# A four-layer transformer step on one core: the linear layer's numerators as sixteen 32x32 tiles, two scratch sets for VectorE, and a newly planned order

## The chip, the cores and the metric

One core of a Trainium2 chip runs the whole program. The metric is the device time of one execution in microseconds; the kernel before takes 2145.01 us (median of 3 runs, 2144.82 to 2145.63).

## The reference, cut to what matters

Two kinds of layers alternate, A, B, A, B, on one sequence of 2048 rows of 1024 elements, in bf16. Each has 32 heads of 32 elements, its layer norm ahead and a residual sum behind it. A is linear attention: a softmax feature map of q and k, a 64x32 state per head, and a quotient. B is full softmax attention.

```python
def _A_ref(x, wqkv, w_phi, wo):
    q, k, v = ...                                        # (B, 32 heads, S, 32)
    pq, pk = einsum("bhsd,hdf->bhsf", q, w_phi), einsum("bhsd,hdf->bhsf", k, w_phi)
    phi_q = concatenate([softmax(pq), softmax(-pq)], axis=-1)      # phi_k alike
    kv = einsum("bhsf,bhsd->bhfd", phi_k, v)
    z  = einsum("bhsf->bhf", phi_k)
    num = einsum("bhqf,bhfd->bhqd", phi_q, kv)
    den = einsum("bhqf,bhf->bhq", phi_q, z)[..., None] + 1e-6
    return (num / den).transpose(...).reshape(B, S, D) @ wo
def _B_ref(x, wqkv, wo):
    p = softmax(einsum("bhqd,bhkd->bhqk", q, k) * Dh ** -0.5)
    return einsum("bhqk,bhkd->bhqd", p, v).transpose(...).reshape(B, S, D) @ wo
x = x + _A_ref(layernorm(x), ...)
x = x + _B_ref(layernorm(x), ...)
x = x + _A_ref(layernorm(x), ...)
x = x + _B_ref(layernorm(x), ...)
```

## The kernel before, in words

The program runs the pair A, B twice (`layer` 0 and 1). The 2048 rows are four chunks `c` of 512. Activations stand transposed (channels on the partitions, rows along the free dimension), so that most matrix products are 128x128 by 512. Four heads fill 128 partitions; such a group of four is `g` in B, and `a` within a half `hf` in A's queries.

Nothing is ordered by hand. Each piece of work is recorded with its engine, a cost in microseconds, its buffers, the pieces it depends on and a priority (`Sched.op`). `Sched.run` then plays a clock through the five engines: whenever an engine is free, it takes the ready piece of lowest priority number whose buffers can be had, under quotas for each kind of buffer (`QUOTA`). The order in which pieces are taken is the order in which instructions are written for each engine. Some rules look at the state of that clock, and some pieces (the score products of B) are created while it runs. A page of constants sets priorities, distances and limits.

**A's keys** (`a_keys`, `a_state`): projections of k and v, exponentials, and the state `kv` and `z`. The state is put into `kvm` as block-diagonal 128x128 matrices (L895 zeroes it on POOL, L899 copies the blocks on VectorE).

**A's queries** (`a_queries`, for each chunk and half, four groups `a` of four heads): the projection (L600), two exponentials each (L972), the sums of them (L983), a ratio of the two softmax denominators through logarithms (L989 to L995) that `split_hl` and `spread` (L935) spread over the partitions, four multiplications on VectorE (L1000), and then for each `a` the numerators: two 128x128 by 512 products with `kvm` (L1010), copied out of PSUM by ScalarE (L1014). The denominators (L1021) go the same way through `spread`, and four multiplications (L1032) give the rows that `a_out` projects with `wo`.

**B's attention** (`attention`): work goes by turns, one turn being a chunk of queries `qc` and a group `g`, 32 turns per layer. A turn has 64 units, a unit being the scores of one head's 128 keys with 512 queries (L1209, a 32-row tile of the array). Scores of two or three units lie side by side in PSUM, and ScalarE turns them into exponentials with one instruction of 1024 or 1536 columns (L1267). A further unit per group can be given to VectorE: L1354 converts it, and for each pair of converted units a chain of four instructions finishes the exponential (`exp_dve`: two masks L1171 into `work`, a product L1176 into `work`, a sum L1176 out of `work`). `work` is one scratch set, held from the first mask to the sum (the buffer `xx`, with one place). TensorE multiplies the results with v and with ones (L1397), VectorE copies the sums out (L1412, twice a turn), and DMAs and VectorE make the quotient. Under the attention lie the projections of B's keys, queries and values (L604), and under that of layer 0 also three chunks of A's keys for layer 1. When TensorE has nothing to do, the planner lets it multiply constants (L604 with `onesD`, L1649, L1654).

How many units VectorE gets is decided while the order is planned, by VectorE's load and by the constants `MOST`, `MIX`, `LOAD`, `THIRD_LOAD`, `BOTH_LOAD`.

## Time and profile before

| what | us |
|---|---|
| median of 3 runs (lowest, highest) | 2145.01 (2144.82, 2145.63) |
| the profiled execution, its own time | 2143.52 |
| its span in the profile | 2141.7 |
| TensorE busy in the span | 2097.4 |
| ScalarE busy | 1929.9 |
| VectorE busy | 1720.8 |
| first and last start of a B exponential (L1267) | 319.1 and 2129.3 |

"Busy" of TensorE counts a product until its modelled end, and products overlap, so 98% does not say that it is full; how closely products follow each other does. Stages by the trace: A's keys to about 155 us, A's queries and B's first projections to 319, attention of layer 0 to about 1171, the rest of layer 1's A to about 1372, attention of layer 1 to 2131, and the last rows. In the attention the copies L1412 mark the turns: copy 1 starts at 345.1 us, copy 32 at 747.2, copy 48 at 958.3, copy 63 at 1160.9, copy 65 (layer 1) at 1401.1, copy 96 at 1769.5 and copy 126 at 2121.3.

### The profile page before, as it was taken

How to read it: one execution, taken by the hardware profiler on the slowest of the kernel's cores; microseconds unless marked ns; L12 is line 12 of the kernel's file. 1: busy time of each engine (PE TensorE's matmuls, PEld its weight loads, DVE VectorE, ACT ScalarE, POOL GpSimd, SP SyncE). 2: the span in 40 equal slices, each digit the busy share in tenths (PEclk: the TensorE clock that was granted, in tenths of full speed). 3: DMA queues.
4: the chain of work that ended last, by engine and by line, in shares of the span. 5: the costliest groups of instructions: out<-in, count | busy, mean ns of one | idle time of the engine just before them, and what ended most of it. 6: DMA issues, size and time to landing. Idle time of an engine off the chain costs nothing.

```text
span 2141.7 us, 64212 instructions
## 1 busy us (share of the span) xinstructions
PE 2097.4 (98%) x27375; PEld 795.1 (37%) x27437; DVE 1720.8 (80%) x3151; ACT 1929.9 (90%) x2044; POOL 27.4 (1%) x78
## 2 busy tenths in 40 slices
PE   8999999999999999999999999999999999999999
PEld 5543443333333333333333434533333333333333
DVE  8876553665567899997887876599899999999998
ACT  7437668999999999999999576799999999999998
POOL 1000000000000000000000000000000000000000
PEclk9999999999999999999999999999999999999999
DMA  7820321112233431451456212211111122311111
GB/s 233 164 71 20 86 63 32 32 42 49 65 99 85 123 107 52 120 154 47 108 154 194 78 40 69 70 28 31 36 49 38 45 53 54 84 39 52 54 44 37
DMA packets 255271, 160.73 MB, mean 75 GB/s; under 512 B 147592, under 2 KB 229512, under 8 KB 254984
## 3 DMA queue, kind: packets, MB, share of 16 engines
q1 hardware_dynamic: 254984, 156.62, 27.3%
q8 instruction: 214, 3.51, 0.7%
q14 instruction: 73, 0.60, 0.1%
HBM read 89.72 MB, written 29.87 MB: 56 GB/s over the span
## 4 chain that ended last, share of the span: by engine, by line
PE 57%; ACT 26%; DVE 9%; issue 5%; DMA 2%; POOL 0%; SPq 0%; ACTq 0%; DVEq 0%; POOLq 0%
ACT arena L1267 26%; PE psum L600 19%; PE psum L604 13%; PE psum L1397 11%; PE psum L1209 10%; DVE arena L1354 3%; DVE work L1171 1%; PE psum L1010 1%; DVE work L1176 1%; DVE arena L1176 1%; DMA arena<-rd 1%; DMA arena<-arena 1%; PE psum L855 1%; ACT arena L820 1%; PE psum L935 1%
## 5 line engine op out<-in xcount | busy, mean ns | idle before, releaser
L1267 ACT ACTIVATE arena<-psum 128x1536 bf16<-128x1536 f32 (+1 forms) x1343 | 1580.5, 1478 | 4.7 <-PE psum L1209 2.9
L604 PE MATMUL psum<-arena 128*32 128x512 bf16 (+1 forms) x9536 | 633.1, 365 | 4.2 <-DVE arena L816 1.0
L1397 PE MATMUL psum<-arena 128*32 128x512 bf16 x4096 | 607.5, 382 | 1.9 <-DVE arena L1412 1.6
L1397 PE MATMUL psum<-arena,ones_bf 128*32 128x512 bf16 x4096 | 607.7, 382 | 0.0
L1209 PE MATMUL psum<-arena 32*128 32x512 bf16 x4096 | 527.2, 383 | 25.7 <-ACT arena L1267 20.6
L1354 DVE TENSOR_SCALAR arena<-psum 128x512 uint16<-128x512 f32 x610 | 415.1, 686 | 117.6 <-PE psum L1209 112.9
L600 PE MATMUL psum<-arena 128*128 128x512 bf16 (+1 forms) x1916 | 429.6, 372 | 4.3 <-issue 1.8
L1209 PEld LDWEIGHTS <-arena 32*128 32x128 bf16 x4096 | 161.1, 91 | 559.2 <-issue 555.2
L604 PEld LDWEIGHTS <-arena 128*32 128x32 bf16 x9536 | 206.1, 95 | 255.3 <-issue 161.9
L600 PEld LDWEIGHTS <-arena 128*128 128x128 bf16 x1968 | 186.4, 98 | 215.4 <-issue 17.1
L1397 PEld LDWEIGHTS <-arena 128*32 128x32 bf16 x4096 | 167.2, 95 | 211.6 <-issue 144.0
L1171 DVE TENSOR_SCALAR work<-arena 128x1024 uint16<-128x1024 uint16 (+1 forms) x616 | 237.7, 418 | 5.7
L1176 DVE TENSOR_TENSOR arena<-work 128x1024 bf16<-128x1024 bf16 (+1 forms) x308 | 209.9, 682 | 5.5
L1176 DVE TENSOR_TENSOR work<-arena,work 128x1024 bf16<-128x1024 bf16 (+1 forms) x308 | 209.1, 679 | 0.1
L1397 PEld LDWEIGHTS <-ones_bf 128*32 128x32 bf16 x4096 | 165.9, 95 | 19.1 <-issue 3.3
L820 ACT ACTIVATE arena<-psum 128x512 bf16<-128x512 f32 x80 | 43.6, 595 | 74.4 <-PE psum L600 61.5
L1073 DVE CAST arena<-psum 128x512 bf16<-128x512 f32 (+1 forms) x120 | 69.5, 579 | 41.0 <-PE psum L604 41.0
L824 DVE TENSOR_REDUCE arena<-arena 128x32 f32<-128x1024 bf16 x64 | 77.6, 1213 | 21.4 <-ACT arena L820 21.0
L1412 DVE COPY arena<-psum 128x512 f32<-128x512 f32 x126 | 86.3, 685 | 10.0 <-PE psum L1397 9.8
L972 ACT ACTIVATE arena<-psum 128x512 bf16<-128x512 f32 x112 | 62.0, 605 | 30.4 <-PE psum L600 26.0
L833 DVE TENSOR_TENSOR arena<-psum,arena 128x1024 bf16<-128x1024 f32 x64 | 78.1, 1222 | 5.3 <-PE psum L604 3.1
L645 ACT ACTIVATE arena<-xR 128x1024 bf16<-128x1024 bf16 x40 | 42.3, 1058 | 30.9 <-DVE xR L1047 30.2
(99 smaller groups left out, 1048.4 us busy)
## 6 DMA issues: line engine op xcount, KB each, us to landing
arena<-in_B_wqkv_dram SPq DMA_DIRECT2D x66, 256.0 KB
arena<-rd SPq DMA_DIRECT2D x62, 256.0 KB
xa<-arena SPq DMA_DIRECT2D x48, 256.0 KB
arena<-in_A_wqkv_dram SPq DMA_DIRECT2D x40, 256.0 KB
arena<-in_B_wo_dram SPq DMA_DIRECT2D x40, 256.0 KB
arena<-arena SPq DMA_DIRECT2D x256, 32.0 KB
arena<-wd_k SPq DMA_DIRECT2D x32, 256.0 KB
arena<-arena SPq DMA_DIRECT2D x62, 128.0 KB
```

Source lines behind the costliest of these rows:

```text
L600: nc.tensor.matmul(out_, lhsT=lhsT, rhs=rhs, start=start, stop=stop, skip_group_check=True)
L604: nc.tensor.matmul(out_[ks, :], lhsT=lhsT[:, ks], rhs=rhs, start=start, stop=stop, tile_position=(0, 32 * k), skip_group_check=True)
L824: red = op("DVE", dve_us(1024) + 0.107, lambda ev=ev, sv=sv: nc.vector.reduce_sum(out=sv(), in_=ev().rearrange("p s (h d) -> p (s h) d", d ...
L833: ml = op("DVE", dve_us(1024), lambda vpv=vpv, wv_=wv_, sv=sv: nc.vector.tensor_tensor(out=wv_()[:, :, :, 0:DH], in0=vpv().rearrange("p (h ...
L1073: return soon(op("DVE", dve_us(n), lambda: nc.vector.tensor_copy(out=dst(), in_=src()), [dep], bufs, prio))
L1171: return sch.later("DVE", n * C512 / 3840 + 0.065, lambda: nc.vector.tensor_scalar(out=out_().bitcast(U16), in0=y_v().bitcast(U16), scalar ...
L1176: return sch.later("DVE", n * C512 / 1920 + 0.065, lambda: nc.vector.tensor_tensor(out=out_(), in0=in0(), in1=in1(), op=what), deps, [e_b, ...
L1209: nc.tensor.matmul(out=out_, lhsT=kT[g][1]()[r, pp, d * P:(d + 1) * P], rhs=q_of[(qc, g)][1]()[r, (pp + j // 2) % 2, :], start=True, stop= ...
L1267: ex = make("ACT", act_us(w * C512), lambda: nc.scalar.activation(out=e_v()[:, 0:w * C512], in_=s_v()[:, 0:w * C512], func=ACT.Exp, scale= ...
L1354: pair["got"].append(sch.later("DVE", dve_us(512), lambda: nc.vector.tensor_scalar(out=e_v().bitcast(U16)[:, k, :], in0=s_v(), scalar1=EXP ...
L1397: nc.tensor.matmul(out=a_v()[col:col + 32, :], lhsT=v_v()[:, kc % 4, o:o + DH] if what == 0 else ones_bf[:], rhs=ev()[:, x * C512:(x + 1) ...
L1412: cp = op("DVE", dve_us(512), lambda t_v=t_v, a_v=a_v: nc.vector.tensor_copy(out=t_v(), in_=a_v()), [last], [a_b, t_b], prio - 4)
```

## The change

**Numerators.** `kvm` is no longer block-diagonal but holds the 32x32 blocks alone, written by one VectorE copy per layer (before: a POOL memset and four copies). For each half there is one piece of work of 32 products, each a 32x32 tile of the array by 512 columns: for both feature halves `s`, four groups `a` and four row quarters `r`, from rows 32r to the output quarter (r + a) mod 4. So each `a` has a PSUM bank of its own, whose four quarters are written from four different row quarters, and within one `s` the sixteen products have sixteen different tiles. The heads of group `a` thereby stand turned by `a` quarters. To match, the denominators are spread with a turned constant (`selr`, seven small POOL copies at the start), and `wo` is loaded turned (`turned_slab`: 14 DMAs per layer in place of 8). The piece waits for all four multiplications of its half, where before each `a` waited for its own, and takes four banks at once.

**Scratch.** `work` has two sets, and `xx` two places. The arena shrinks from 170 to 166 KB per partition for it.

**Order.** Planner rules and a good half of the constants change. In layer 1 the four evacuations of chunk 3's transposed rows go from ScalarE to VectorE (`COPY`). Some new code is switched off by its constants: `send` (`FAR` is 0), pooled banks (`POOL` is 0), VectorE evacuations (`EVAC` is 4).

```diff
+                    if (e == "PE" and self.wants is not None and item[3].accum is not None and item[3].bufs[0].at is None
+                            and self.live.get("E", 0) < self.open):
+                        shut = item
+                        skipped.append(item)
+                        continue
...
-SBUF_ARENA = 170 * 1024
+SBUF_ARENA = 166 * 1024
...
-MIX = (lambda i: (2, 2, 1, 2)[i // 8], lambda i: (0, 0, 1, 0)[i // 8])
-LOAD = (2.24, 2.19)
+MIX = (lambda i: (1, 2, 1, 0)[i // 8], lambda i: (0, 0, 1, 0)[i // 8])
+LOAD = (2.16, 2.38)
...
-    work = const.tile([P, 2, max(NB), C512], BF16, tag="work")
+    work = const.tile([P, 2, 2, max(NB), C512], BF16, tag="work")
...
+    def turned_slab(prio, src):
+        b, v = sb("slab", PO, C512)
+        got = []
+        for a in range(4):
+            n = 32 * a
+            got.append([dma(prio, lambda a=a, at=at, of=of: nc.sync.dma_start(
+                out=v()[at, a::4, :], in_=src[of, a::4, :]), (), [b], kb=2 * (at.stop - at.start), bulk=True)
+                for at, of in ((slice(n, P), slice(0, P - n)), (slice(0, n), slice(P - n, P))) if at.stop > at.start])
+        return b, v, [got[0] + got[1], got[2] + got[3]] * 2
...
-        m_b, kvm = sb("kvm", 16, P)
+        m_b, kvm = sb("kvm", 16, DH)
...
-        for a in range(4):
-            g = 4 * hf + a
-            n_b, n_v = ps("num", ANY)
-
-            def fn(a=a, g=g, n_v=n_v):
+        for lo in range(0, 4, NUM):
+            held = [ps("num", ANY) for _ in range(NUM)]
+            held[0][0].with_ = tuple(b for b, _ in held[1:])
+
+            def fn(lo=lo, held=held):
                 for s in range(2):
-                    nc.tensor.matmul(n_v(), lhsT=kvm()[:, 2 * g + s, :], rhs=eq[a][1]()[:, s, :],
-                                     start=(s == 0), stop=(s == 1))
-            nm = op("PE", 2 * MM, fn, [ew[a]] + state, [n_b, m_b, eq[a][0]], prio, mode="n")
...
+                    for a in range(lo, lo + NUM):
+                        for r in range(4):
+                            rows, at = slice(32 * r, 32 * r + 32), 32 * ((r + a) % 4)
+                            nc.tensor.matmul(held[a - lo][1]()[at:at + 32, :], lhsT=kvm()[rows, 2 * (4 * hf + a) + s, :],
+                                             rhs=eq[a][1]()[rows, s, :], start=(s == 0), stop=(s == 1),
+                                             tile_position=(32 * r, at), skip_group_check=True)
+            nm = op("PE", NUM_US, fn, ew[lo:lo + NUM] + state, [b for b, _ in held] + [m_b] + [eq[a][0] for a in range(lo, lo + NUM)],
+                    prio, mode="x")
...
-        x_b = Buf("ps", 0, "xx", [(8,)])
+        x_b = Buf("ps", 0, "xx", [(8,), (9,)])
```

How instructions move shows at two places. The first is ScalarE in the middle of A's queries of layer 0. Before: L972 are exponentials of the projections, L1014 the copies of the numerators, L989, L991 and L995 the ratio, L1026 and L1028 the denominators, L645 the next layer norm.

```order
L972 ACTIVATE arena<-psum 128x512 x4
L1014 COPY arena<-psum 128x512
L972 ACTIVATE arena<-psum 128x512 x2
L1014 COPY arena<-psum 128x512
L1026 ACTIVATE arena<-psum 128x512
L989 ACTIVATE arena<-psum 128x512
L1028 ACTIVATE arena<-arena 128x512
L991 ACTIVATE arena<-psum 128x512
L1014 COPY arena<-psum 128x512
L995 ACTIVATE arena<-arena 128x512
L1014 COPY arena<-psum 128x512
```

The changed kernel at the same place (L1038 are the exponentials, L1085 the copies of the numerators, L1097 and L1099 the denominators, L1055 to L1061 the ratio, L683 and L685 the layer norm):

```order
L1038 ACTIVATE arena<-psum 128x512 x4
L1085 COPY arena<-psum 128x512 x4
L1097 ACTIVATE arena<-psum 128x512
L1055 ACTIVATE arena<-psum 128x512
L1099 ACTIVATE arena<-arena 128x512
L1057 ACTIVATE arena<-psum 128x512
L683 ACTIVATE arena<-xR 128x1024
L685 ACTIVATE arena<-xR 128x1024
L1061 ACTIVATE arena<-arena 128x512
```

The four copies, which lay between other work one by one, now follow each other, ahead of the denominators.

The second place is VectorE in the late turns of layer 0's attention, between copies 55 and 56. Before: L1354 converts a unit, L1171 are masks, L1176 the product into `work` and the sum out of it, L1459 a quotient.

```order
L1176 TENSOR_TENSOR arena<-work 128x1024
L1354 TENSOR_SCALAR arena<-psum 128x512
L1171 TENSOR_SCALAR work<-arena 128x1024 x2
L1176 TENSOR_TENSOR work<-arena,work 128x1024
L1354 TENSOR_SCALAR arena<-psum 128x512
L1459 TENSOR_TENSOR arena<-arena 128x512
L1176 TENSOR_TENSOR arena<-work 128x1024
L1354 TENSOR_SCALAR arena<-psum 128x512
```

The changed kernel, between the same two copies (L1241 are masks, L1246 the product and the sum, L1436 converts, L1541 is the quotient):

```order
L1241 TENSOR_SCALAR work<-arena 128x1024
L1246 TENSOR_TENSOR work<-arena,work 128x1024
L1241 TENSOR_SCALAR work<-arena 128x1024
L1246 TENSOR_TENSOR arena<-work 128x1024
L1541 TENSOR_TENSOR arena<-arena 128x512
L1241 TENSOR_SCALAR work<-arena 128x1024
L1246 TENSOR_TENSOR work<-arena,work 128x1024
L1241 TENSOR_SCALAR work<-arena 128x1024
```

The next pair's mask now stands between a chain's product and its sum, and the chains stand closer together.

Counted over the whole orders: B's exponentials on ScalarE are 1332 instructions for 3434 units, before 1343 for 3486; VectorE converts 662 units, before 610. By stretches between the copies L1412 (units left to ScalarE, before and after): copies 1 to 32, 890 and 875; 32 to 48, 431 and 428; 48 to 63, 423 and 397; the whole of layer 0, 1808 and 1764; the whole of layer 1, 1678 and 1670, in 664 and 651 instructions. Numerator products on TensorE are 512 of 32x32, in 16 pieces, before 128 of 128x128; in the changed order 12 to 30 of the 128x128 products L638 stand between the last spreading of the ratio and the piece of numerators that waits for it, in seven of the 16 pieces just 12 at most (12 five times, once 10 and once 4, the last two with half of the spreading some products earlier).

245 lines of the change are left out of this document (151 added, 94 removed).

## The prediction

> **What bounds the kernel now.** I read the page first: the busy shares and the 40 slices.
>
> ```profile
> span 2141.7 us, 64212 instructions
> ...
> DVE  8876553665567899997887876599899999999998
> ACT  7437668999999999999999576799999999999998
> POOL 1000000000000000000000000000000000000000
> PEclk9999999999999999999999999999999999999999
> ```
>
> ScalarE (ACT) is full from slice 8 to slice 22 and again from slice 27 on: those are the two attentions. VectorE (DVE) has room in the first half of the first attention, little at its end, and none to speak of in the second. The granted clock is level, so nothing is throttled. Next the busy times by stretch, cut where a turn's copy L1412 marks the place: the first A queries, then the attention of layer 0 in three stretches (copies 1, 32, 48, 63), the second A queries, and the attention of layer 1 in two. Columns are the stretch, its length, and each engine's busy time.
>
> ```profile
> 155.00:319.10 164.10, 162.66 (x878) 69.05 (x888) 94.60 (x185) 116.48 (x225) 0.00 (x0) 1.00 0.21 54
> 345.10:747.20 402.10, 398.06 (x5600) 132.53 (x5598) 257.55 (x466) 402.10 (x333) 0.00 (x0) 1.00 0.27 68
> 747.20:958.30 211.10, 204.85 (x3039) 70.37 (x3039) 198.20 (x354) 209.92 (x199) 3.99 (x11) 1.00 0.37 108
> 958.30:1160.90 202.60, 196.27 (x3211) 70.57 (x3207) 166.94 (x289) 200.97 (x185) 6.16 (x14) 1.00 0.38 109
> 1245.00:1371.60 126.60, 125.84 (x741) 59.89 (x752) 76.49 (x156) 91.30 (x186) 0.00 (x0) 1.00 0.28 72
> 1401.10:1769.50 368.40, 365.64 (x5681) 134.80 (x5678) 350.50 (x677) 368.29 (x328) 0.00 (x0) 1.00 0.17 41
> 1769.50:2121.30 351.80, 340.62 (x4655) 112.02 (x4656) 341.38 (x644) 351.80 (x304) 0.00 (x0) 1.00 0.19 52
> ```
>
> In the attentions ScalarE is busy 99 to 100% of every stretch, so its sum is their length. In the two query stretches it is busy 71 and 72%, VectorE 58 and 60%, TensorE 99%. TensorE's figure counts overlap, so I looked at how its products follow each other there, in the timeline (start, length, line, count):
>
> ```profile
> 160.64 0.59 PE L1010 MATMUL psum<-arena 128*128 128x512 bf16 x2
> 161.07 1.46 PE L600 MATMUL psum<-arena 128*128 128x512 bf16 x6
> 162.37 0.59 PE L1010 MATMUL psum<-arena 128*128 128x512 bf16 x2
> 162.89 0.61 PE L1021 MATMUL psum<-arena 128*32 128x512 bf16 x8
> 163.34 0.60 PE L983 MATMUL psum<-arena,rep 128*32 128x512 bf16 x8
> ```
>
> Two full products take 0.43 us (160.64 to 161.07), six take 1.30, and the next work starts at once. From full to column tiles the step is 0.52 for two, so a change of tiling costs 0.09. Eight column tiles take 0.45: four run side by side. TensorE sets the length of the query stretches; every product taken away there is time.
>
> **Numerators.** Before, 64 products per layer (16 for each of the four chunks) at 0.2165 are 13.9 us, in the full tiling like their neighbours. Now there are eight pieces per layer of 32 small products. No row shows 32x32 tiles. The nearest are four column tiles (above), row tiles of the scores, and the short column tiles of A's state:
>
> ```profile
> 1728.53 0.39 PE L1209 MATMUL psum<-arena 32*128 32x512 bf16 x3
> 1728.85 0.39 PE L1397 MATMUL psum<-arena 128*32 128x512 bf16 x1
> ```
>
> ```profile
> 69.72 1.38 PE L855 MATMUL psum<-arena 128*32 128x33 bf16 x128
> ```
>
> Three row tiles and a change of tiling take 0.32, so row tiles overlap as well as column tiles, and a weight load with its short product is issued every 1.38 / 128 = 0.011 us. If both overlaps hold together, a piece is two passes of sixteen, 0.43, plus the 0.16 in which sixteen are issued, plus one more change of tiling, 0.1: 0.69. Eight are 5.5, and a layer saves 8.4, both layers 16.8. If only four overlap at once, as in every row, the piece is 8 x 0.2165 + 0.1 = 1.83, and both layers lose 1.6. I take 16.8: rows show overlap in either direction, the issue rate suffices, and the turned heads give each product of a pass its own tile. The Trainium skill, "TensorE: Matmul & The Clock Gate", Part 3, gives 10.6 times for sixteen such tiles; no run here shows it. By that figure a piece would be 0.75 and the gain some 1 us smaller (an estimate).
>
> The piece now waits for all four multiplications of its half.
>
> ```profile
> 182.84 0.40 PE L935 MATMUL psum<-arena,selb 32*128 32x512 bf16 x4
> ```
>
> ```profile
> 183.26 2.48 DVE L1000 TENSOR_TENSOR arena<-arena,psum 128x512 bf16<-128x512 bf16 x4 [0.74 <-PE psum L935]
> ```
>
> They end 2.9 us after the spreading starts (182.84 to 185.74). In the order mostly 12 to 18 products L638 stand between: 12 x 0.2165, and 0.32 for the spreading with its change of tiling as for the scores, are 2.9. That cover is just enough; where it is short by 0.3, sixteen pieces cost 5 us at most, and behind the waiting piece stand the denominators and everything else on TensorE. ScalarE's four copies in a row are four of the same instructions in another place; with ScalarE a quarter idle I cost them at nothing, and the four banks that they hold likewise. They would cost what TensorE then waits for a bank.
>
> **State, constants, loads.**
>
> ```profile
> L899 DVE CAST arena<-arena 32x512 bf16<-32x512 f32 x8 | 3.3, 418 | 0.1
> ```
>
> ```profile
> 108.71 3.65 SPq L700 DMA_DIRECT2D arena<-in_A_wo_dram  x7
> ```
>
> ```profile
> 185.96 0.69 DVE L1047 TENSOR_TENSOR xR<-xR,psum 128x512 bf16<-128x512 bf16 x1 [0.23 <-PE psum L600]
> ```
>
> Four copies of 0.42 and a POOL memset become one copy per layer; projections keep TensorE busy meanwhile. `wo` takes six more DMAs per layer on SP's queue, at 3.65 / 7 = 0.52 some 3 us of issue; in layer 0 they come at 109 us, and the first sum that needs them starts at 186. `selr` is set by seven small POOL copies at the start, behind which stands the memset of `phi`, itself ahead of loads; at a microsecond or so it would show as a later start of the fold, which I cost at nothing since the keys wait for their own DMAs as well. Four evacuations go from ScalarE to VectorE in the second query stretch, where neither is the bound. All nothing; at worst 2 us.
>
> **Fewer units on ScalarE.** The price of a unit comes from the groups kept apart by form, and from one run of the same form:
>
> ```profile
> L1267 ACT ACTIVATE arena<-psum 128x1536 bf16<-128x1536 f32 x801 | 1196.3, 1650 | 4.0 <-PE psum L1209 2.2 <-DMA xa<-arena 1.1 <-PE psum L1397 0.6
> L1267 ACT ACTIVATE arena<-psum 128x1024 bf16<-128x1024 f32 x541 | 619.6, 1223 | 0.7 <-PE psum L1209 0.7
> ```
>
> ```profile
> 329.86 22.94 ACT L1267 ACTIVATE arena<-psum 128x1536 bf16<-128x1536 f32 x17 [1.59 <-PE psum L1209]
> ```
>
> A unit more makes an instruction 1650 - 1223 = 427 ns longer. Seventeen take 22.94, of which the last is 1.65: one follows another every 1.33. So an instruction costs 0.05 + 0.427 per unit. By the counts of the orders, with ScalarE as the bound: copies 1 to 32 lose 15 units, 6.4 us; copies 32 to 48 three, 1.3; copies 48 to 63 twenty-six, 11.1; layer 1 eight units and 13 instructions, 4.1. Together 22.9.
>
> **What VectorE pays.** A unit more on VectorE, and the single scratch set, by the timeline in the second attention:
>
> ```profile
> 1705.28 0.68 DVE L1176 TENSOR_TENSOR arena<-work 128x1024 bf16<-128x1024 bf16 x1
> 1705.99 0.76 DVE L1171 TENSOR_SCALAR work<-arena 128x1024 uint16<-128x1024 uint16 x2
> 1706.67 0.68 DVE L1176 TENSOR_TENSOR work<-arena,work 128x1024 bf16<-128x1024 bf16 x1
> 1707.39 0.69 DVE L1176 TENSOR_TENSOR arena<-work 128x1024 bf16<-128x1024 bf16 x1
> 1708.11 0.43 DVE L1171 TENSOR_SCALAR work<-arena 128x1024 uint16<-128x1024 uint16 x1
> 1708.46 0.68 DVE L1354 TENSOR_SCALAR arena<-psum 128x512 uint16<-128x512 f32 x1
> 1709.06 0.68 DVE L1085 TENSOR_SCALAR arena<-psum 128x512 bf16<-128x512 f32 x1
> ```
>
> A conversion takes 0.60 (1708.46 to 1709.06), two masks 0.68. A product followed by its own sum takes 0.72, and a sum followed by the next mask 0.71 to 0.72: 0.12 more than the 0.60 of work that waits for nothing. With two sets the second of these waits goes, and the first goes where something stands between. A unit is 0.60 + (0.68 + 2 x 0.60) / 2 = 1.54. In layer 1 the order has 88 products right ahead of their sums and 70 sums right ahead of a mask before, 29 of the first now: 129 x 0.12 = 15 us saved, against eight units, 12 us. VectorE's load there stays, and ScalarE's 4.1 stand.
>
> In layer 0, copies 1 to 32 have 145 us of idle VectorE for 15 units, 23 us: hidden. Copies 48 to 63 have 35.7 idle for 26 units, 40 us, less 0.12 for some 20 waits that go, as near as the order tells. VectorE would then be busy some 205 of a stretch that lasts 202.6 and that ScalarE alone would end in 191.5. So VectorE becomes the bound there and the 11.1 do not come. Copies 32 to 63 together hold 365 us of it before and some 407 now, in 413.7; the best share it reaches in a long stretch is 341.4 of 351.8, 97%. At that share the stretch takes 420, 6 longer; full, it takes 407, 7 shorter. I take no change for it, in the middle.
>
> **The sum**, against the profiled execution (2143.5, span 2141.7 and 1.8 around it; 1.5 under the median of the runs): 16.8 + 6.4 + 0 + 4.1 = 27.3, so 2116, and some 2117 on the scale of the median. About 0.2%, 4 us, is what a measurement can tell from no change.
>
> **Rivals.**
>
> *Quarters of one bank collide* (6%). Four row tiles in succession write four quarters of the same bank. If products from different row quarters could not write one bank at the same time, the 32 would run one by one: 32 x 0.2165 = 6.9 a piece, 111 for sixteen in place of 27.7: 83 slower. With 10.5 gained in the attentions that is 2143.5 + 83 - 10.5, by the median 2218. It turns slower once a piece takes over 1.73 + 10.5 / 16 = 2.4 us, which is fewer than three products at once. For it: the scores' row tiles and the spreading always write different banks, so no row contradicts it. Against it: four column tiles write the quarters of one bank side by side (L1021), and the quarters are different partitions. The Trainium skill, "TensorEngine Tiling (Array Packing)", Restrictions and Gotchas, states it: "Different row tiles cannot access same PSUM bank simultaneously". By that rule this rival would be the result.
>
> *Four at a time* (9%). Tiles in both directions overlap no better than in one: numerators lose 1.6 where 16.8 were to be gained, 2143.5 + 1.6 - 10.5 = 2135, or 2136 by the median. For it: no row has more than four.
>
> *VectorE as the bound of the late first attention* (17%): at 97% it adds 6, and the cover of the numerators may be short by up to 2: 2125. For it: 97% is the most that VectorE reaches in a stretch where ScalarE is full. Against it: part of its busy time there is the 0.12 waits that now go.
>
> *ScalarE remains the bound throughout* (14%): VectorE's added work fits by the shorter chains, the 12.4 come too, 2105. For it: ScalarE is the bound in every attention stretch now. Against it: 205 of VectorE's work do not go into 191.5, unless parts of it move over the stretch's ends.
>
> *The order's waits* (8%): transfers or buffers land later than planned, in an arena 4 KB smaller; anywhere from 2125 to 2165, slower in a quarter of it, the same in half. For it: TensorE and ScalarE both run with next to no gap, so any late buffer shows. Against it: the DMA share is 13 to 38% in those stretches.
>
> **How the numbers follow.** The forecast has 46%. Faster by over 0.2%: 46 + 9 + 17 + 14 + 2 = 88%; same 4%; slower 6 + 2 = 8%. The range reaches from the full ScalarE gain with ScalarE's 2.8 idle of the two late stretches closed as well and a microsecond or two of the same kind elsewhere, 2100, to four at a time, 2137; colliding banks and the worst of the waits lie outside.
>
> **What would show it.** Right: the group of L1078 has its pieces 0.6 to 0.8 apart from the next work, the query stretch of layer 0 is some 8 us shorter with TensorE still without gaps, ScalarE stays full between copies 1 and 32, and between copies 48 and 63 it shows idle time ended by TensorE whose products wait for VectorE. Wrong: pieces of 1.8 or 6.9 us; idle TensorE ahead of L1078, released by VectorE's L1065; VectorE with room left in the late turns; or ScalarE with gaps in the second attention.

## The result, and the profile after

The changed kernel takes 2132.30 us (median of 5 runs, 2129.46 to 2136.92); beside it the kernel before took 2144.82 (5 runs, 2143.44 to 2145.63). The ratio is 0.9943 [0.9929, 0.9958]: faster by 0.6%, 12.5 us where the forecast had 28, and inside the range. The profiled run is the longest of the five, 2136.92, so its terms are set against each other here and not against the median.

The page of the changed kernel first, the slices that answer to those of before:

```profile
span 2135.1 us, 65137 instructions
...
DVE  8866545757566899999998876698899999999998
ACT  7437769989999999999999577799999999999998
...
PEclk9999999999999999999999999999999999999999
...
L1338 ACT ACTIVATE arena<-psum 128x1536 bf16<-128x1536 f32 (+1 forms) x1332 | 1559.3, 1437 | 28.0 <-PE psum L1280 20.0
```

ScalarE has an 8 in the first attention where it had 9s, and the last line has 28.0 us of idle time ahead of the exponentials, 20.0 of it ended by the scores L1280. The same groups had 4.7 in the kernel before. The busy times by the same stretches (query stretches, copies 1 to 32, 32 to 48, 48 to 63, second queries, and layer 1 from its copy 65), then the time between the first exponentials of the two layers, the linear stage between the attentions, and layer 1 from its first exponential to its last copy:

```profile
155.00:310.20 155.20, 154.58 (x1087) 64.62 (x1080) 93.70 (x185) 114.74 (x225) 0.00 (x0) 1.00 0.21 57
334.30:744.60 410.30, 402.43 (x5617) 135.11 (x5613) 278.94 (x511) 398.32 (x334) 0.00 (x0) 1.00 0.26 66
744.60:959.80 215.20, 206.99 (x3077) 70.34 (x3074) 200.06 (x363) 207.35 (x197) 4.98 (x12) 0.99 0.38 109
959.80:1163.90 204.10, 197.90 (x3218) 70.31 (x3217) 200.43 (x370) 198.47 (x190) 4.65 (x12) 1.00 0.41 108
1245.00:1369.10 124.10, 123.89 (x912) 57.48 (x910) 80.06 (x163) 87.13 (x181) 0.00 (x0) 0.99 0.28 73
1398.10:1764.40 366.30, 361.53 (x5683) 135.61 (x5675) 344.74 (x680) 365.96 (x318) 0.00 (x0) 1.00 0.16 40
1764.40:2113.50 349.10, 339.54 (x4643) 112.90 (x4644) 344.01 (x663) 349.10 (x301) 0.00 (x0) 1.00 0.19 53
...
310.20:1369.10 1058.90, 1034.08 (x13933) 375.80 (x13931) 822.73 (x1503) 958.22 (x1007) 12.45 (x32) 0.99 0.32 87
...
1170.90:1369.10 198.20, 195.85 (x1688) 88.74 (x1680) 134.93 (x252) 130.63 (x268) 2.81 (x8) 0.99 0.30 82
1369.10:2113.50 744.40, 729.17 (x10732) 258.32 (x10733) 717.68 (x1397) 743.80 (x645) 0.00 (x0) 1.00 0.18 46
...
606.00:608.00 2.00, 0.46 (x9) 0.11 (x6) 1.70 (x3) 1.39 (x2) 0.00 (x0) 1.00 0.40 91
608.70:612.10 3.40, 3.40 (x34) 0.80 (x30) 0.00 (x0) 2.53 (x2) 0.00 (x0) 0.51 0.12 25
```

The last three of these long stretches in the kernel before:

```profile
319.10:1371.60 1052.50, 1033.66 (x13708) 379.34 (x13730) 767.04 (x1370) 977.42 (x1010) 12.86 (x33) 1.00 0.32 87
1170.90:1371.60 200.70, 198.91 (x1436) 92.63 (x1447) 134.73 (x251) 134.81 (x273) 2.72 (x8) 1.00 0.28 78
1371.60:2121.30 749.70, 734.69 (x10766) 257.33 (x10768) 719.70 (x1373) 748.91 (x658) 0.00 (x0) 1.00 0.17 45
```

Added up, from the profiled executions:

| stretch | before | after | forecast | measured |
|---|---|---|---|---|
| start to first exponential | 319.1 | 310.2 | -8.4 | -8.9 |
| to copy 1 | 26.0 | 24.1 | 0 | -1.9 |
| copies 1 to 32 | 402.1 | 410.3 | -6.4 | +8.2 |
| copies 32 to 48 | 211.1 | 215.2 | 0 | +4.1 |
| copies 48 to 63 | 202.6 | 204.1 | 0 | +1.5 |
| copy 63 to layer 1's first exponential | 210.7 | 205.2 | -8.4 | -5.5 |
| layer 1, first exponential to last copy | 749.7 | 744.4 | -4.1 | -5.3 |
| rest | 20.4 | 21.6 | 0 | +1.2 |
| span | 2141.7 | 2135.1 | -27.3 | -6.6 |

ScalarE did lose its work: between the first exponentials of the two layers it is busy 958.2 us in place of 977.4. But that stretch is 6.4 us longer (1058.9 against 1052.5): these 19 us, and the 8.4 of layer 1's numerators that lie in it too, were given back, and 6.4 more. Part of that is the clock: the last two rows of the changed kernel's windows show TensorE idle for 1.5 us at 606 and then a granted clock of 0.51 for 3.4 us. Four such pieces (at 608.7, 871.5, 1165.0 and 1246.9; after its first 15 us the kernel before has none) take up to 1.7 us of TensorE's work each. The run with these four has the lowest mean clock of the five (0.996) and is the longest; the one with the highest (0.999) is the shortest, 2129.46.

The pieces themselves, in the changed kernel's timeline, and the place where copies 1 to 32 lose most:

```profile
162.40 0.65 PE L1078 MATMUL psum<-arena 32*32 32x512 bf16 x32
162.98 0.61 PE L1092 MATMUL psum<-arena 128*32 128x512 bf16 x8
...
463.63 8.45 ACT L1338 ACTIVATE arena<-psum 128x1536 bf16<-128x1536 f32 x6
...
471.34 1.90 PE L642 MATMUL psum<-arena 128*32 128x512 bf16 x32
...
473.29 0.69 DVE L1155 TENSOR_SCALAR arena<-psum 128x512 bf16<-128x512 f32 x1 [2.12 <-PE psum L642]
...
475.04 0.50 SPq L1160 DMA_DIRECT2D arena<-arena  x1
475.59 0.59 SPq L1161 DMA_DIRECT2D arena<-arena  x1
...
479.07 0.59 PE L1280 MATMUL psum<-arena 32*128 32x512 bf16 x4 [0.98 <-DMA arena<-arena]
...
479.54 3.71 ACT L1338 ACTIVATE arena<-psum 128x1536 bf16<-128x1536 f32 x3 [7.46 <-PE psum L1280]
```

Thirty-two products take 0.58 us until the next work starts (162.40 to 162.98). From 469.8 to 477.7 TensorE has projections (L642) and weighted sums (L1479) and no scores, and ScalarE stands still for 7.46 us. The chain behind it is in the rows: the next turn's queries are projected, VectorE scales them (L1155), two transfers of SP turn them (L1160, L1161), and the scores wait for these. The order itself has 7.88 us of such work in a row at this place (469.82 to 477.70). Two sets of scores in succession start 8.2 us apart here; in the kernel before, never more than 2.4 between copies 1 and 63.

### The profile page after: what moved, and what is told of

It is laid out like the page before. It is cut to its first block, busy times and chain, and to the rows that moved or that the text cites. A ratio compares the mean times of both kernels' runs of the same rounds, so it can differ in the third digit from the quotient of the medians.

```text
span 2135.1 us, 65137 instructions
## 1 busy us (share of the span) xinstructions
PE 2086.7 (98%) x27811; PEld 787.5 (37%) x27811; DVE 1772.2 (83%) x3305; ACT 1904.7 (89%) x2029; POOL 26.6 (1%) x83
## 5 line engine op out<-in xcount | busy, mean ns | idle before, releaser
L1338 ACT ACTIVATE arena<-psum 128x1536 bf16<-128x1536 f32 (+1 forms) x1332 | 1559.3, 1437 | 28.0 <-PE psum L1280 20.0
L642 PE MATMUL psum<-arena 128*32 128x512 bf16 (+1 forms) x9536 | 634.6, 366 | 10.7 <-DVE arena L1212 2.6
L1479 PE MATMUL psum<-arena 128*32 128x512 bf16 x4096 | 606.3, 383 | 1.8 <-DVE arena L1494 1.4
L1479 PE MATMUL psum<-arena,ones_bf 128*32 128x512 bf16 x4096 | 606.4, 383 | 0.0
L1280 PE MATMUL psum<-arena 32*128 32x512 bf16 x4096 | 524.5, 384 | 24.9 <-ACT arena L1338 17.6
L1436 DVE TENSOR_SCALAR arena<-psum 128x512 uint16<-128x512 f32 x662 | 444.8, 681 | 80.9 <-PE psum L1280 76.6
L638 PE MATMUL psum<-arena 128*128 128x512 bf16 (+1 forms) x1968 | 430.5, 373 | 0.9 <-DMA arena<-in_A_wqkv_dram 0.4
L1280 PEld LDWEIGHTS <-arena 32*128 32x128 bf16 x4096 | 160.5, 91 | 551.8 <-issue 548.1
L642 PEld LDWEIGHTS <-arena 128*32 128x32 bf16 x9536 | 209.4, 95 | 262.2 <-issue 163.9
L638 PEld LDWEIGHTS <-arena 128*128 128x128 bf16 x1968 | 185.9, 98 | 220.4 <-issue 22.1
L1241 DVE TENSOR_SCALAR work<-arena 128x1024 uint16<-128x1024 uint16 (+1 forms) x668 | 261.8, 414 | 2.3
L1479 PEld LDWEIGHTS <-arena 128*32 128x32 bf16 x4096 | 167.7, 95 | 213.1 <-issue 146.9
L1246 DVE TENSOR_TENSOR arena<-work 128x1024 bf16<-128x1024 bf16 x334 | 225.7, 676 | 2.6
L1246 DVE TENSOR_TENSOR work<-arena,work 128x1024 bf16<-128x1024 bf16 x334 | 225.5, 675 | 0.0
L1479 PEld LDWEIGHTS <-ones_bf 128*32 128x32 bf16 x4096 | 166.1, 95 | 22.3 <-issue 4.0
L1038 ACT ACTIVATE arena<-psum 128x512 bf16<-128x512 f32 x112 | 60.7, 617 | 26.4 <-PE psum L638 22.5
L683 ACT ACTIVATE arena<-xR 128x1024 bf16<-128x1024 bf16 x40 | 42.4, 1065 | 36.4 <-DVE xR L1117 36.4
```

The costliest lines, as they stand in the source:

```text
L638: nc.tensor.matmul(out_, lhsT=lhsT, rhs=rhs, start=start, stop=stop, skip_group_check=True)
L642: nc.tensor.matmul(out_[ks, :], lhsT=lhsT[:, ks], rhs=rhs, start=start, stop=stop, tile_position=(0, 32 * k), skip_group_check=True)
L1241: return sch.later("DVE", n * C512 / 3840 + 0.065, lambda: nc.vector.tensor_scalar(out=out_().bitcast(U16), in0=y_v().bitcast(U16), scalar ...
L1246: return sch.later("DVE", n * C512 / 1920 + 0.065, lambda: nc.vector.tensor_tensor(out=out_(), in0=in0(), in1=in1(), op=what), deps, [e_b, ...
L1280: nc.tensor.matmul(out=out_, lhsT=kT[g][1]()[r, pp, d * P:(d + 1) * P], rhs=q_of[(qc, g)][1]()[r, (pp + j // 2) % 2, :], start=True, stop= ...
L1338: ex = make("ACT", act_us(w * C512), lambda: nc.scalar.activation(out=e_v()[:, 0:w * C512], in_=s_v()[:, 0:w * C512], func=ACT.Exp, scale= ...
```

## The experiments

All ratios are to the kernel before, run beside each kernel. Where one leaves work out, its expectation says so.

**Turned or not.** The output quarter is made the same as the row quarter, so that each half's products fall on four tiles of the array, eight on each, in place of sixteen. The heads come out in the wrong quarters.

```diff
-                            rows, at = slice(32 * r, 32 * r + 32), 32 * ((r + a) % 4)
+                            rows, at = slice(32 * r, 32 * r + 32), 32 * r
```

> The changed kernel with the 32 products of a piece on the four diagonal tiles alone (row quarter r to output quarter r, heads not turned), so that only four can run at a time; every instruction stands where it stood, and the heads land in the wrong quarters. Theory (sixteen side by side, TensorE bounds the query stretches): a piece goes from 0.58 to about 1.75 us, sixteen of them cost 18 to 19 us, 2132 becomes 2150. Rival (the query stretches are bound by something else, and the tiles' speed is hidden): pieces as long, but the time within 5 us of 2132.

Measured: 2150.44 (11 runs, 2144.75 to 2152.84), 1.0021 [1.0011, 1.0030], 18.1 above the changed kernel. Its timeline:

```profile
162.46 1.91 PE L1078 MATMUL psum<-arena 32*32 32x512 bf16 x32
164.30 0.40 PE L1092 MATMUL psum<-arena 128*32 128x512 bf16 x4
```

A piece takes 1.84, the price of the rival "four at a time" (1.83). The first exponential comes at 318.8 (changed kernel 310.2), the stage between the attentions takes 206.6 (198.2): 8.6 and 8.4, on either layer. So sixteen tiles side by side, against four, are worth 18 us here, and the mechanism of the sum's largest term holds. Read against the kernel before, this run is the rest of the change at nearly the old price of the numerators (1.84 against 8 x 0.2165 = 1.73 a half): by the medians it is 5.6 us slower.

**A shorter product on VectorE in the late turns.** The product of each chain takes 64 of a unit's 512 columns in the last eight turns of the first attention.

```diff
+            w = 64 if what == ALU.mult and 470 <= prio < 560 else C512
...
-                out=out_(), in0=in0(), in1=in1(), op=what), deps, [e_b, x_b], prio)
+                out=out_()[:, :, 0:w], in0=in0()[:, :, 0:w], in1=in1()[:, :, 0:w], op=what), deps, [e_b, x_b], prio)
```

> The changed kernel with VectorE's product of each exponential chain cut from 512 to 64 columns per unit in the last eight turns of the first attention (prio 470 to 560); same order, the values of those units are wrong. It takes some 23 us off VectorE between copies 48 and 63 and nothing off any other engine. Theory (VectorE bounds that stretch): the stretch falls from 204 towards ScalarE's 192, the total by 8 to 12, to about 2122. Rival (VectorE's work is covered, ScalarE or TensorE is the bound, or late transfers): within 3 us of 2132, the stretch at 202 to 204.

Measured: 2130.26 (2128.52 to 2134.12), 0.9933 [0.9921, 0.9946]. Copies 48 to 63 in its windows:

```profile
959.20:1162.50 203.30, 197.60 (x3218) 70.02 (x3219) 184.40 (x371) 197.22 (x190) 4.55 (x12) 1.00 0.39 108
```

VectorE is busy 184.4 in place of 200.4 (16 us less, where 23 were expected) and the stretch is 0.8 shorter. VectorE was not its bound.

**The late units back on ScalarE.** `MIX` for the last quarter of the first attention, 71 conversions on VectorE there in place of 97.

```diff
-MIX = (lambda i: (1, 2, 1, 0)[i // 8], lambda i: (0, 0, 1, 0)[i // 8])
+MIX = (lambda i: (1, 2, 1, 2)[i // 8], lambda i: (0, 0, 1, 0)[i // 8])
```

> The changed kernel with the fourth value of MIX in the first attention set back from 0 to 2: the order is the same for the first 23 turns, then VectorE converts 71 units in the last eight turns in place of 97. Theory (VectorE bounds those turns, the 26 units bring nothing): the stretch of copies 48 to 63 stays at 202 to 205, total 2129 to 2135. Rival (ScalarE is the bound and the units were a gain): 11 us more in that stretch, total about 2143.

Measured: 2140.17 (10 runs, 2137.96 to 2142.95), 0.9977 [0.9968, 0.9986]: 7.9 slower than the changed kernel. Its windows, copies 48 to 63, and from copy 48 to the last exponential of layer 0, here and in the changed kernel:

```profile
955.50:1158.60 203.10, 194.66 (x3184) 69.45 (x3181) 163.30 (x284) 201.70 (x184) 4.32 (x12) 1.00 0.39 111
955.50:1171.20 215.70, 205.42 (x3317) 72.88 (x3318) 169.58 (x292) 212.40 (x192) 4.32 (x12) 0.99 0.41 118
...
959.80:1170.90 211.10, 204.72 (x3297) 72.32 (x3299) 206.04 (x377) 202.60 (x193) 4.65 (x12) 0.99 0.42 115
```

Copies 48 to 63 are no longer than in the changed kernel (204.1), as the theory had it, but the median goes the rival's way: the time lies behind copy 63. To the last exponential ScalarE has 9.8 us more work and the time is 4.6 longer. So in this order the late units, which I had at nothing, were worth 4.6 by the profiles and 7.9 by the medians, of their 11.1; the runs do not tell which.

**One scratch set.** `xx` has one place again; the order is planned anew by that.

```diff
-        x_b = Buf("ps", 0, "xx", [(8,), (9,)])
+        x_b = Buf("ps", 0, "xx", [(8,)])
```

> The changed kernel with one scratch set in use (xx has one place), planned anew; the first 16 turns are the same. Theory (each sum followed by a mask waits 0.12, VectorE is full in the late first and in the second attention): some 35 waits in the late turns and 70 in the second attention, 4 to 12 us slower, 2136 to 2144. Rival (the second set only moves waits about): within 3 us of 2132.

Measured: 2179.49 (4 runs), 1.0162 [1.0147, 1.0176]. Its windows, the stage between the attentions and the first half of layer 1's:

```profile
1162.90:1408.90 246.00, 225.93 (x2303) 104.29 (x2321) 154.69 (x276) 136.40 (x277) 4.06 (x12) 0.98 0.35 95
1437.10:1813.20 376.10, 366.57 (x5722) 137.77 (x5719) 347.46 (x672) 372.69 (x324) 0.00 (x0) 1.00 0.17 40
```

The first half of layer 1 is 9.8 longer (376.1 against 366.3), the whole of it 8.1 (752.5 against 744.4). Of this, 5.0 is work of ScalarE's own (748.8 against 743.8): planned anew, the order leaves it nine units more. The larger part of the loss, 48 us between the attentions, is another thing: the planner put work there that it otherwise fits into the attention (2303 products in place of 1688). This run weighs the scratch set only in layer 1, and there together with these units.

**The tiles alone**, in the kernel before with its own costs and one scratch set (the diff is the changed kernel's `a_queries`, `turned_slab`, `selr` and five quotas).

> The kernel before with the small tiles alone: the numerators, the turned heads and the four queues' numbers that belong to them; one scratch set, and the costs by which the kernel before was planned, so that its units go to ScalarE and VectorE almost as before (253 conversions on VectorE in the first attention, 360 in the second, no stretch of TensorE over 2.1 us without scores). Theory (what was lost is lost by the order of the first attention, whose turns hold little free time on TensorE): the tiles' 16.8 arrive whole and nothing is given back, 2128 (2125 to 2131): less than the changed kernel's time though it moves no unit off ScalarE; copies 1 to 32 take 402 to 404. Rival (the tiles themselves lose 8 us again in the first attention, by their four banks or their waits): copies 1 to 32 take 408 to 411 here as well, 2134 to 2137.

Measured: 2131.02 (2128.41 to 2135.83), 0.9933 [0.9919, 0.9946]: the whole gain of the change, with hardly a unit moved (253 conversions in the first attention, 250 before). Its windows, copies 1 to 32 and the time between the layers' first exponentials:

```profile
337.50:740.00 402.50, 398.01 (x5600) 133.15 (x5597) 257.88 (x466) 402.46 (x333) 0.00 (x0) 1.00 0.27 68
...
313.40:1363.30 1049.90, 1026.98 (x13896) 374.83 (x13894) 766.89 (x1374) 976.46 (x1010) 11.19 (x32) 1.00 0.32 87
```

Copies 1 to 32 are as before the change, so the tiles are not what costs there. The gain, 13.9, is some 3 short of 16.8.

**More of the first turns on ScalarE.** The hole at 470 goes from the order.

```diff
-MIX = (lambda i: (1, 2, 1, 0)[i // 8], lambda i: (0, 0, 1, 0)[i // 8])
+MIX = (lambda i: (2, 2, 1, 0)[i // 8], lambda i: (0, 0, 1, 0)[i // 8])
```

> The changed kernel with one number of the order altered: the planner may mix two units in place of one into a turn's start in the first quarter of the layer. Its order then has no stretch of 7.88 us without scores on TensorE at the start of the thirteenth turn; the longest is 3.1, in the twentieth. The first eight turns hold 48 conversions in place of 61. Theory (the bare stretch of the order costs what it lasts): ScalarE's idle time of copies 1 to 32 falls from 12.0 to 4 to 6, that stretch takes 402 to 405 in place of 410, and the time is 2124 to 2128. Rival (TensorE is full over the whole of these turns, and a hole closed at one place opens at another): copies 1 to 32 still take 408 to 411, the time is 2129 to 2134.

Measured: 2169.87 (4 runs), 1.0119 [1.0105, 1.0133]: neither theory's time. Its windows, copies 1 to 32, 48 to 63, and the stage behind:

```profile
334.20:741.10 406.90, 399.47 (x5622) 133.40 (x5620) 259.64 (x470) 403.21 (x333) 0.00 (x0) 1.00 0.26 66
957.20:1146.60 189.40, 183.10 (x2683) 61.01 (x2683) 184.28 (x346) 182.74 (x176) 4.11 (x9) 0.98 0.29 83
1155.70:1401.80 246.10, 229.01 (x2366) 105.55 (x2358) 157.48 (x281) 136.18 (x277) 4.48 (x13) 1.00 0.33 98
```

ScalarE's idle time in the first row falls from 12.0 to 3.7, as the theory of the hole has it, for 3.4 us. But 14.7 us won in copies 48 to 63 are paid with 47.9 behind the attention. That was not expected by either theory, and is the subject of the run before the last.

**A quarter of the projections left out**, in the changed kernel and in the kernel before, with the orders otherwise kept.

```diff
                 for po in range(at, at + step):
+                    if cols and 200 <= prio < 545 and lo == 0 and hi == 4 and po in (3, 4):
+                        continue
```

> The changed kernel, whose query, key and value projections under the first attention leave out a quarter of their products (two of eight; the sums are partial; 2480 products, 134 us of TensorE at 0.2165 for four); the order is the same otherwise. Theory (with fewer units on ScalarE, TensorE bounds the first attention): ScalarE's idle time between copies 1 and 63 falls from 25.5 to under 8, copies 1 to 32 take 398 to 403, copies 32 to 63 408 to 414, and the time is 2108 to 2118. Rival (the order's places and transfers make ScalarE wait, not TensorE's load): idle time stays over 15 and the time over 2124.

> The kernel before with the same products left out, for comparison. ScalarE is full there in the whole first attention (idle 2.8 of 816), so both theories expect next to nothing between copies 1 and 63 (0 to 3 us less), and 2139 to 2145. If TensorE sets the pace there as well, it falls by more than 5.

Measured: 2123.86 (4 runs), 0.9905 [0.9892, 0.9919], for the changed kernel; 2145.47 (11 runs), 1.0006 [0.9998, 1.0015], for the kernel before. The changed kernel so lightened, copies 1 to 32, and the waits of ScalarE from copy 1 to copy 63:

```profile
333.40:741.20 407.80, 375.48 (x4982) 128.52 (x4979) 279.25 (x511) 398.24 (x334) 0.00 (x0) 1.00 0.26 67
```

```profile
ACT arena L1340 <- PE psum L1282: 13.9, 12, 7.2
```

The kernel before gains nothing: as long as ScalarE is full, TensorE's load does not show. In the changed kernel, whose ScalarE has less to do, 134 us of products fewer are worth 8.4 us by the medians. By the profiles 8.6 us go in copies 32 to 63 (410.7 in place of 419.3). But copies 1 to 32 lose 2.5 and no more, ScalarE's idle time from copy 1 to 63 falls only to 17.3, and the one wait of 7.2 stays: there it is the place of the queries in the order and their two transfers, not TensorE's load. My theory fell for the first stretch and held for the later ones (408 to 414 expected); the idle time, 17.3, is the rival's (over 15), and the total lies just under the rival's 2124.

**Layer 0 ordered as before the change.** Small tiles, two scratch sets and layer 1's numbers stay; the costs and due times that order layer 0 are those of the kernel before (`MIX`, `LOAD`, `MOST`, `THIRD_LOAD`, `BOTH_LOAD`, `BEHIND` and `NEAR` for layer 0; `SLACK` and the due times of projections and loads, some of which serve both layers).

```diff
-MIX = (lambda i: (1, 2, 1, 0)[i // 8], lambda i: (0, 0, 1, 0)[i // 8])
-LOAD = (2.16, 2.38)
+MIX = (lambda i: (2, 2, 1, 2)[i // 8], lambda i: (0, 0, 1, 0)[i // 8])
+LOAD = (2.24, 2.38)
...
```

> The changed kernel with the numbers that order layer 0 set back to those of the kernel before (the planner's costs and due times for the first attention); small tiles, two scratch sets and the numbers of layer 1 stay. Its order has 253 conversions on VectorE in the first attention (before 250, changed kernel 298), none of the stretches without scores over 2.1 us, and 366 in the second. Theory (TensorE is as full as ScalarE between the first exponentials of the two layers, so the units moved there brought nothing and the new order's holes cost): copies 1 to 32 take 402 to 404, layer 1 keeps its 5 us, and the time is 2124 to 2128, below both kernels. Rival (units off ScalarE did help, only hidden by waits): without them the time is 2132 or more.

Measured: 2129.96 (2128.14 to 2131.15), 0.9931 [0.9918, 0.9943]. Windows, copies 1 to 32, and between the first exponentials:

```profile
334.70:736.80 402.10, 397.14 (x5593) 132.86 (x5590) 257.08 (x466) 402.10 (x332) 0.00 (x0) 1.00 0.27 68
...
310.60:1360.70 1050.10, 1024.40 (x13861) 375.16 (x13886) 764.81 (x1378) 972.60 (x1005) 12.62 (x32) 1.00 0.32 88
```

Copies 1 to 32 are back at 402.1 with no idle time. The median is the lowest of all whole kernels here, by 2.3 under the changed kernel; the intervals of the two overlap, so "below both" is shown against the kernel before only, and the median is 2 above the theory's range. Copies 32 to 63 hold 6.2 us of ScalarE idle here (417.7 in place of 413.7 in the kernel before). Forty-five conversions fewer on VectorE, with the units back on ScalarE, cost nothing in the median.

**Its late units off ScalarE again**, by one number:

```diff
-MIX = (lambda i: (2, 2, 1, 2)[i // 8], lambda i: (0, 0, 1, 0)[i // 8])
+MIX = (lambda i: (2, 2, 1, 0)[i // 8], lambda i: (0, 0, 1, 0)[i // 8])
```

> The kernel of the run ahead of it, with one number more: in the last quarter of the first attention units for VectorE may follow one another without a turn of ScalarE's between. 93 conversions there in place of 68, 29 more in the layer; the order now puts 72 projections and the rest of a fold (128 short products) behind the attention, where the order's longest stretch without scores grows from 195 to 219 us. Theory (TensorE's work is the sum that must be done between the first exponentials of the two layers): the attention gets 10 to 14 us shorter and the stretch behind it 20 to 28 longer, so the time is 6 to 16 longer than that of the run ahead. Rival (ScalarE alone sets the length): 10 to 13 us shorter than the run ahead.

Measured: 2150.18 (10 runs, 2148.14 to 2151.06), 1.0023 [1.0014, 1.0033], 20 slower than the run ahead: the theory's direction, a little beyond its range. Windows, copies 48 to 63, the stage behind the attention, and between the first exponentials:

```profile
947.40:1139.10 191.70, 186.52 (x2753) 64.00 (x2750) 188.10 (x350) 187.58 (x179) 3.21 (x9) 1.00 0.33 93
1146.40:1378.30 231.90, 219.31 (x2096) 101.11 (x2118) 150.70 (x271) 134.02 (x274) 3.76 (x11) 0.99 0.33 94
...
309.90:1378.60 1068.70, 1039.88 (x13959) 380.97 (x13985) 806.23 (x1462) 961.47 (x1007) 11.91 (x32) 1.00 0.32 86
```

and the projections in the stage behind, in the run ahead and in this one (count, busy time, mean):

```profile
L642 PE MATMUL psum<-arena 128*32 128x512 bf16 x84 | 5.4, 380 | 0.0
```

```profile
L642 PE MATMUL psum<-arena 128*32 128x512 bf16 x384 | 26.0, 410 | 5.5 <-DVE arena L891 1.7 <-DVE arena L1212 1.5 <-DVE arena L874 0.8
```

From copy 1 to the last exponential it is 16 us shorter, for 29 units of 0.427, and the stage behind is 35 longer: 300 products more stand there (75 times four, 16 us), and waits and fillers around them, since nothing else is left to do. ScalarE is busy 11 us less between the first exponentials, and that time is 18.6 longer. Full as ScalarE is, it does not set the length alone.

**Late weights.** The 256 KB loads issued by GpSimd in place of SP.

```diff
-            return b, v, [dma(prio, lambda: nc.sync.dma_start(out=v(), in_=src), deps, [b], kb=256, bulk=True)] * 4
+            return b, v, [dma(prio, lambda: nc.gpsimd.dma_start(out=v(), in_=src), deps, [b], kb=256, bulk=True)] * 4
```

> The changed kernel, with the loads of the second layer's projection weights (256 KB each) issued by GpSimd in place of SP, so that they stand behind nothing on SP's queue; order otherwise the same. Theory (weights that land 1.5 us late at 605 and 868 let TensorE idle, and each such gap is followed by 3.41 us at half clock): two of the four halvings go, 2128 to 2130, with a smaller spread. Rival (the gaps have other causes): 2131 to 2134, halvings as before.

Measured: 2130.69 (2128.01 to 2135.20), 0.9937 [0.9924, 0.9949], between the two theories' times; the spread is the same. Windows, the place of the changed kernel's first halving, and another:

```profile
608.70:612.10 3.40, 3.40 (x53) 1.17 (x46) 1.21 (x3) 3.40 (x4) 2.29 (x3) 1.00 0.53 126
...
798.00:804.00 6.00, 5.92 (x62) 1.58 (x61) 2.85 (x6) 3.28 (x3) 0.33 (x1) 0.72 0.06 21
```

The weight that TensorE waited for at 606 is issued at 592.0 in place of 602.1; the wait is gone, and the clock behind it is full. But that does not show that the late weight cost the halving: in the unturned run TensorE waited 2.25 us for the same weight (at 615.0), and the clock stayed full behind it. The edit does not reach the other place of the theory: between 680 and 900 us no load of this kind is issued in either kernel. TensorE's gap there stays, and this time no halving follows it:

```profile
868.04 0.40 PE L642 MATMUL psum<-arena 128*32 128x512 bf16 x4 [1.69 <-issue]
```

Half clock comes elsewhere in this profile, for 3.4 us at 799.7 and for 6.8 at 1240.0. What late weights cost in the median is below what this run can tell.

## Why the prediction was right in part, and where it failed

**Numerators: right.** A piece was to take 0.69 and takes 0.58: two passes of sixteen at 0.2165 are 0.43, and a change of tiling and a little more the rest. Layer 0's query stretch is 8.9 shorter (forecast 8.4). The cover ahead of the pieces held: no wait stands ahead of L1078. Four row quarters write four quarters of one bank without waiting for each other, so the rival of the colliding quarters (6.9 a piece) is out, as is "four at a time", whose price shows only where the heads are not turned. In the old order the tiles brought 13.9 of the 16.8. The Trainium skill, "TensorEngine Tiling (Array Packing)", Restrictions and Gotchas, has "Different row tiles cannot access same PSUM bank simultaneously"; the trace does not agree for different quarters of a bank, by the 0.58 of a piece.

**Numerators in layer 1: right in mechanism, smaller in size.** The unturned run shows the full 8.4 there as well. Only 2.5 of it arrive between the attentions (198.2 against 200.7). The profiled run has one halving of the clock in that stage (at 1246.9), 1.7, and TensorE is idle for 2.4 where it was 1.8. The unturned run, at nearly the old price of the numerators, takes 5.9 longer there than the kernel before (206.6 against 200.7), so it is not the tiles' speed that fell short. But the tiles alone, in the old order, gain no more than 3.2 there (197.5). What in that stage costs the 3.6 that remain stays open.

**Layer 1's attention: right.** Forecast 4.1, measured 5.3, with ScalarE still full (365.96 of 366.30, 349.10 of 349.10).

**Copies 1 to 32: the step that failed.** The prediction took ScalarE to stay the bound there ("with ScalarE as the bound: copies 1 to 32 lose 15 units, 6.4 us") and asked only if VectorE could hide its share: "copies 1 to 32 have 145 us of idle VectorE for 15 units, 23 us: hidden". VectorE did hide them (278.9 busy of 410.3). But ScalarE did not stay the bound: its idle time goes from 0.0 to 12.0 and the stretch becomes 8.2 longer in place of 6.4 shorter. That is 14.6 of the 20.7 us by which the profiled run falls short of the sum (by the medians it is 15.5 short). The other profiles of this order agree: 409.5 in the unturned run and 409.3 with the late units back, both without half clock in the stretch. That the new order is the cause and not the tiles show the two kernels with the old order there (402.5 and 402.1), and that TensorE's load is not the main cause shows the lightened kernel (407.8). Of the 12.0, 7.5 are ScalarE's wait at 472 and 2.0 one at 530.6; the 1.05 and 1.24 that it waits around 608 come with a late weight and the clock. At 472 the rows show how it comes: ScalarE is through with a turn's scores, and the next turn's queries, whose projection, scaling and two transfers come one behind the other, are not ready. That units taken off ScalarE are what brings this about, because they use up a turn's scores sooner, is argued and not shown by itself.

**Copies 48 to 63: near in size, by a wrong reason.** "So VectorE becomes the bound there and the 11.1 do not come": a shorter product on VectorE moved the end by 0.8 us, so VectorE is not the bound. That the stretch hardly changed was luck. Nor do the 26 units lie there. By the starts in the traces ScalarE has 8 units fewer between these two copies (407, before 415); 12 are missing between copies 32 and 48 (426, before 438) and 12 behind copy 63 (11, before 23). The written orders, from which the prediction counted, do not say where ScalarE stands when VectorE makes a copy. The stretch also holds new waits for scores (5.6 us of ScalarE idle, 1.6 before).

**What stood against ScalarE's terms in layer 0** was in the table that the prediction quotes (TensorE 398.06 of 402.1). The prediction followed TensorE's products one by one in the query stretches only. By counts from the kernel before, copies 1 to 32, apart by form:

```profile
L604 PE MATMUL psum<-arena 128*32 128x512 bf16 x2512 | 180.0, 382 | 0.7 <-DVE arena L1101 0.2 <-DVE arena L1085 0.2
L1397 PE MATMUL psum<-arena,ones_bf 128*32 128x512 bf16 x992 | 149.0, 382 | 0.0
L1397 PE MATMUL psum<-arena 128*32 128x512 bf16 x992 | 149.0, 382 | 0.1
L1209 PE MATMUL psum<-arena 32*128 32x512 bf16 x996 | 129.4, 383 | 3.3 <-ACT arena L1267 2.5
```

Column tiles four at a time and scores three at a time are (2512 + 992 + 992) / 4 + 996 / 3 = 1456 times 0.2165, 315 us, and two changes of tiling of 0.09 around each of 332 sets of scores 60 more: 375 of 402.1, 93%. That the little room left must lie just where scores are due is my reading. What the runs show: less load on TensorE gave back 8.6 us in copies 32 to 63 and 2.5 in copies 1 to 32, and 29 units taken off ScalarE in the last run of that kind sent 300 projections behind the attention, for 20 us.

**The rivals.** "The order's waits" (8%, 2125 to 2165) comes nearest, by its time and in part by its mechanism: two transfers do end waits of TensorE, the turned queries at 479 (0.98) and a weight at 607.7 (1.54). But most of the longest wait, 7.5, stood in the order as planned; only the last of it was for a transfer. "ScalarE remains the bound throughout" and "VectorE as the bound" are out by their own rows. What stays open is how the 13.8 us by which copies 1 to 63 grew split between the planner's constants: they were changed together, and setting one back moved other work as well.

## What to carry to other kernels

When a planned order has two engines above 90%, count the second one's work by number and spacing before taking load off the first, and look in the new order for the longest stretch in which the first gets nothing: here 7.9 us of it were to be read before any run. A change of an operation and a new order are two changes; the operation alone, in the old order, gave the whole gain. And when a piece gets faster on one engine, follow the inputs of the next piece back, to the projection and its transfers, and ask if they come sooner too.

## What the runs showed of the hardware

Sixteen 32x32 tiles run side by side, also into quarters of one bank: 32 products of 512 columns in 0.58 us with a change of tiling, against 1.84 on four tiles.

In the changed kernel's profile the granted clock fell to half for 3.41 us, one to two us after the end of idle times of TensorE of 1.47 to 2.14 us, at four places. The length of the gap does not decide it: gaps of 1.58 (at 800.0 in the same profile), 2.25 (at 615.0 in the unturned run) and 2.34 (at 607.5 with the late units back) had the full clock behind them. In this profile the starts of half clock lie whole steps of 3.413 us apart: 77.0 steps from 608.7 to 871.5, 86.0 on to 1165.0, 24.0 on to 1246.9. In the step ahead of each, TensorE was busy for 1.86, 1.27, 1.37 and 1.97 of the 3.41 us. The gap of 2.25 falls across two such steps and leaves 2.25 and 2.32 busy in them:

```profile
868.09:871.50 3.41, 1.27 (x19) 0.31 (x13) 1.36 (x3) 1.27 (x3) 0.00 (x0) 1.00 0.76 251
...
612.70:616.11 3.41, 2.25 (x34) 0.65 (x30) 1.92 (x3) 3.41 (x3) 0.00 (x0) 1.00 0.72 161
```

So how much idle time falls into one step seems to count, but no threshold can be read from these runs: 1.83 busy in the step from 799.8 was followed by full clock, and 2.19 ahead of 1055.1, in the run with layer 0 ordered as before, by half. The Trainium skill, "TensorE: Matmul & The Clock Gate", HAM oscillation, speaks of idle gaps over about 3.4 us; here gaps of 1.47 to 2.14 us were followed by half the clock.
